# Attention values and output products in column halves, the row maxima moved into the MLP, and one score bank in four copied out by VectorE

## The chip, the core and the metric

The kernel runs on one core of one Trainium2 chip. The metric is the device time of one execution in microseconds (us). Engines: PE (TensorE, with its weight loads as PEld), ACT (ScalarE), DVE (VectorE), POOL (GpSimd) and SP (SyncE, which here only issues DMAs). A difference of about 0.2% is what a measurement of this kernel can tell from none.

## The reference, cut to what matters

```python
x = A_x                                        # [1, 2048, 448], S = 2048, D = 448
# A: 16 heads of width 28, one key and one value head for all of them
q = (x @ wq).reshape(B, S, 16, 28).transpose(0, 2, 1, 3)
k, v = x @ wk, x @ wv
p = softmax(einsum("bhqd,bkd->bhqk", q, k) * 28 ** -0.5)
a = einsum("bhqk,bkd->bhqd", p, v).transpose(0, 2, 1, 3).reshape(B, S, 448) @ wo
# B: token shift, then an MLP of width F = 1792
h  = gelu(layernorm(x) @ w1)
x1 = x + shifted_quarters(h) @ w2
b  = x1 + gelu(layernorm(x1) @ w3) @ w4
g  = sigmoid((x * gate_w).sum(-1, keepdims=True))
return g * a + (1 - g) * b
```

Everything is float32. The test data make the scores large (`wq` and `wk` are scaled by about 42 and 44), so the softmax needs a shift by something like the row maximum.

## The kernel before

All instruction streams are written out by hand: the order in which the Python code emits an engine's instructions is the order in which that engine runs them (`tc.manual_schedule` for all five engines). The kernel has three stages.

**First stage (0 to about 127 us).** Projections of queries, keys, values and gate, and the token-shift half of B. The queries go to a DRAM tensor `qd`, [4 groups, 128 partitions, 2048 positions]. A group holds four heads, each on 32 partitions: 28 query rows, and four spare rows.

**MLP (about 127 to 402 us).** For each of four blocks `b` of 512 positions, 14 iterations `f` over chunks of 128 of F. An iteration emits `w3_part(b, f)` (11 matmuls of 512 columns, then on ACT two gelus `gh`, `gf` and on DVE the low half `gl = gf - gh`), and, two iterations behind, `w4_part(f - 2, ...)` (12 matmuls of 448 columns into four accumulators). So f = 0 and f = 1 of a block have no `w4_part`. At b = 2, f = 1 the queries of the first unit are loaded and at f = 5 split into high and low halves (`q_split`); at b = 3 two "fills" compute this unit's maxima (`max_all(0)`, `max_end(0)`).

**Attention (402 us to the end).** There are NU = 16 *units*: block `b` of 512 queries times group `g` of four heads. A unit takes NV = 8 *steps*; step k = 8 u + v handles two tiles of 128 keys (kt = 2v and 2v + 1). A step emits, in this order:

- at v = 6, `q_begin(u + 2)` (DVE: a cast and a subtraction of 512 columns, `q_split`) and `q_fetch(u + 3)` (a load of 256 KB);
- for each kt, `scores`: three rounds of four matmuls. The four heads of a round use four row tiles of the array at once and write four PSUM banks. Then `exps`: ACT reads each bank, takes the exponential, and writes a tile `p` in SBUF (L810);
- at v = 2 and v = 3 the reciprocal of the last unit's row sums and its product with the output (`recip`, `norm`), through small DMAs `rt`, `rd` and the broadcast `rb`;
- at v = 2, `max_all(u + 1)` (four matmuls of the queries with 32 of the keys, and a DVE reduction) and `max_end(u + 1)` (three small DVE operations and eight DMAs that write minus the maxima, as two float32r terms, into two spare rows of the queries' SBUF tile `qh`);
- at v = 4 to 7, the output product of the last unit, `wo_job` and `wo_add`: for 128 queries eight matmul instructions of 448 columns in four column tiles, and one DVE addition into `ot`. For unit 0 `w4_job` stands in its place;
- `values` of step k - 1: `vext` (values and a column of ones) times `p`, 16 matmuls of 512 columns in four column tiles into one bank, which DVE copies or adds to `o` (L826, L828).

The maxima need not be exact: they are taken over 32 keys only, row sums beyond a limit are noted (`check`), and the branch `redo` at the end recomputes everything with full maxima in that case.

PSUM has eight banks, kept as a list: `take()` removes the first one, and it is appended again where its last reader is emitted. So a step's banks go round in a fixed order, and a bank's next user waits for its last reader: of the four banks of a key tile for the exponentials, of the bank of `values` for the DVE addition.

The hooks of this change are already there: `READ` is the order in which a key tile's four banks are read, and `DRAIN`, empty before, lists those that DVE copies to SBUF, where `late_exps` takes the exponential in place after both key tiles.

Of the kernel before, what the change touches and what calls it, by code (L numbers as in the profile page):

```python
# [9 lines left out]
F32 = mybir.dt.float32  # L10
F32R = mybir.dt.float32r
AF = mybir.ActivationFunctionType
ALU = mybir.AluOpType
# [23 lines left out]
def f32(ap):  # L37
    return ap.bitcast(F32)
# [3 lines left out]
def gated_mix_kernel(  # L42
# [44 lines left out]
    def misc_tile(name):  # L87
        return psA.tile([P, 512], F32, tag="misc", bufs=1, name=name)
# [105 lines left out]
    mx_of = {}  # L194
    mc_of = {}

# [22 lines left out]

    def max_end(u):  # L220
        mr = mx_of.pop(u).rearrange("p j t -> p (j t)")
        mc = late.tile([P, 32], F32R, tag="mc", bufs=1, name=f"mc_{u}")
        nc.vector.tensor_scalar(mc[:, 0:16], mr, -1.0, None, op0=ALU.mult)
        nc.vector.scalar_tensor_tensor(mc[:, 16:32], mr, -1.0, f32(mc)[:, 0:16],
                                       op0=ALU.mult, op1=ALU.subtract)
        mrow = late.tile([P, 32], F32, tag="mrow", bufs=1, name=f"mrow_{u}")
        nc.vector.transpose(mrow, f32(mc))
        for k in range(2):
            for p in range(4):
                r = 32 * p + 16 * k  # L230
                nc.sync.dma_start(
                    f32(qh_of[u])[DH + k:P:32, :].rearrange("j (t p q) -> p j t q", p=4, q=32)[p], mrow[r:r + 16, :])

# [368 lines left out]
    with tc.tile_pool(name="s2", bufs=1, reuse_waits="tile") as s2, \  # L602
# [4 lines left out]

        fills = [lambda: max_all(0, misc_tile("m_0")), lambda: max_end(0)]

        def fill():  # L610
            if fills:
                fills.pop(0)()

# [25 lines left out]
        for b in range(NB):  # L639
            acc = [ps2.tile([P, 512], F32, tag="acc", bufs=4, name=f"acc_{b}_{t}") for t in range(4)]  # L640
            gs = {}
            for f in range(NF):
# [40 lines left out]
            for t in range(4):  # L683
# [5 lines left out]
            for t in range(4):  # L689
# [3 lines left out]
                nc.vector.tensor_add(xt, xt, acc[t][:, 0:D])  # L693
        assert not fills
    ctx2.close()


    with tc.tile_pool(name="s3", bufs=1, reuse_waits="tile") as s3, \
# [7 lines left out]
        def take():  # L706
            return banks.pop(0)
# [48 lines left out]

        def wo_job(u, t, end=None):
            b, g = divmod(u, NG)
            n = 4 * b + t
            ps = take()  # L760
            for j in range(4):
                tok = slice(t * P + 32 * j, t * P + 32 * j + 32)
                nc.tensor.matmul(ps[32 * j:32 * j + 32, 0:D], on_of[u][:, tok], wof[:, g, :],  # L763
                                 start=True, stop=True, tile_position=(0, 32 * j))
            before = x1[:, n, :] if g == 0 else ot_of[n]
            if g == 0:
                ot_of[n] = s3.tile([P, D], F32, tag="ot", bufs=5, name=f"ot_{n}")
            if end:
                end(t, n, ps[:, 0:D], before)
                banks.append(ps)  # L770
                return
            return n, g, ps, before

        def wo_add(n, g, ps, before):
            nc.vector.scalar_tensor_tensor(ot_of[n], ps[:, 0:D], gg[:, n:n + 1], before, op0=ALU.mult, op1=ALU.add)  # L775
            banks.append(ps)
            if g == NG - 1:
                nc.sync.dma_start(out[0, n * P:(n + 1) * P, :], ot_of[n])

# [37 lines left out]
        def values(u, v, add=True):  # L817
            pv = take()
            for kt in (2 * v, 2 * v + 1):
                ps = p_of.pop((u, kt))  # L820
                for j in range(4):
                    nc.tensor.matmul(pv[32 * j:32 * j + 32, :], vext[:, kt, :], ps[j],  # L822
                                     start=(kt % 2 == 0), stop=(kt % 2 == 1), tile_position=(0, 32 * j))
            if v == 0:
                o_of[u] = s3.tile([P, 512], F32, tag="o", bufs=2, name=f"o_{u}")
                nc.vector.tensor_copy(o_of[u], pv)  # L826
            elif add:
                nc.vector.tensor_add(o_of[u], o_of[u], pv)  # L828
            else:
                return pv  # L830
            banks.append(pv)

        READ = (0, 1, 2, 3)
        DRAIN = ()
        WO_AT = (4, 5, 6, 7)
        M_AT = 2

        for k in range(NU * NV):
            u, v = divmod(k, NV)
            if v == 6 and u + 2 < NU:  # L840
                q_begin(u + 2)
                q_fetch(u + 3)
            for kt in (2 * v, 2 * v + 1):
                exps(u, kt, scores(u, kt))
            for kt in (2 * v, 2 * v + 1):
                late_exps(u, kt)
            if v == 2 and sums:
                norms.append(recip(*sums.pop()))
            if v == 3 and norms:
                norm(*norms.pop())  # L850
            if v == M_AT and u + 1 < NU:
                ps = take()
                max_all(u + 1, ps)
                banks.append(ps)
# [16 lines left out]
        pv = values(u, NV - 1, False)  # L871
# [4 lines left out]
        tq = [bank(f"oq_{t}")[:, 0:P] for t in range(4)]  # L876
        rr = s3.tile([P, 2, 2, 4], F32, name="rr4")
# [33 lines left out]
        def keep_warm(n):  # L911
            for _ in range(n):
                nc.tensor.matmul(banks[0][:, 0:256], warm[:, 0:P], warm, start=True, stop=True)

        for t in range(4):
            nc.vector.tensor_add(o[:, toks[t]], o[:, toks[t]], pv[:, toks[t]])
        with tc.block():
# [34 lines left out]
        with tc.If(again > 0, label="redo"):  # L952
            for b in range(NB):
                for g in range(NG):
# [3 lines left out]
                    max_full(u, bank)  # L958
                    max_end(u)
                    pv = take()  # L960
# [13 lines left out]
                    for t in range(4):  # L974
                        wo_add(*wo_job(u, t))

# [50 lines left out]
```

## Time and profile before

| | |
|---|---|
| median of 3 runs | 971.56 us (971.14 to 971.71) |
| the profiled execution | 970.74 us, of it 968.9 us span |
| granted PE clock, mean | 0.996 |
| PE busy | 960.1 us (99%) |
| PE weight loads (PEld) | 589.3 us (61%) |
| ACT busy | 647.0 us (67%) |
| DVE busy | 345.7 us (36%) |
| POOL busy | 74.9 us (8%) |

A busy PE is not a PE at its peak: matmuls are pipelined, their records overlap, and the interval from one start to the next is what tells the rate. In the two MLP and attention stages the limits differ: the MLP has ACT busy 25% and PEld 87% of the time, attention ACT 93% and PEld 44%.

### The profile page before, as it was taken

Reading aid. Unit: us, or ns where it says so; the run is one execution under the profiler, and the core shown is the slowest. Engines: PE = TensorE matmul, PEld = TensorE weight load, DVE = VectorE, ACT = ScalarE, POOL = GpSimd, SP = SyncE. Lnnn points to the kernel's source line nnn. Section 1 sums busy time; section 2 is a strip of 40 time slices with the busy share of each in tenths; the row PEclk is TensorE's granted clock in tenths of the full one; section 3 lists DMA queues with packets and bytes.
Section 4 is the critical chain, followed back from the end, with each engine's and each line's share of the span. In section 5 each row is a group of like instructions: output and inputs, shape, how many; then the busy total and the mean of one; then the engine's idle time right before and its main releaser. Section 6 shows DMA issues by size and latency. Waiting matters only on the chain. (4 is left out here: it accounts for less than half of the span.)

```text
span 968.9 us, 19222 instructions
## 1 busy us (share of the span) xinstructions
PE 960.1 (99%) x7571; PEld 589.3 (61%) x7571; DVE 345.7 (36%) x636; ACT 647.0 (67%) x1262; POOL 74.9 (8%) x105
## 2 busy tenths in 40 slices
PE   9999999999999999999999999999999999999996
PEld 7788888888888888644444444444444444444442
DVE  5663354433413421233333333333233332333323
ACT  5532444422222222589999999999999999999993
POOL 2242200221002400200000000000000000000000
PEclk9999999999999999999999999999999999999999
DMA  9703342300300300100000010000010000100001
GB/s 317 263 27 76 103 162 83 89 22 10 93 1 1 82 1 1 60 13 14 14 23 14 24 50 24 14 13 24 24 51 15 14 25 13 53 23 2 13 13 42
DMA packets 38753, 46.22 MB, mean 48 GB/s; under 512 B 8880, under 2 KB 27008, under 8 KB 38656
## 3 DMA queue, kind: packets, MB, share of 16 engines
q1 hardware_dynamic: 35632, 39.45, 13.6%
q10 hardware_dynamic: 3024, 5.47, 1.6%
q8 instruction: 61, 1.00, 0.4%
q14 instruction: 36, 0.29, 0.1%
HBM read 32.85 MB, written 11.67 MB: 46 GB/s over the span
## 5 line engine op out<-in xcount | busy, mean ns | idle before, releaser
L810 ACT ACTIVATE p<-bank 128x512 f32<-128x512 f32 x1024 | 510.9, 653 | 42.7 <-PE bank L800 42.7
L822 PE MATMUL bank<-p,vext 128*32 128x512 f32 x2048 | 245.9, 598 | 0.0
L800 PEld LDWEIGHTS bank<-qh,kH 30*128 30x128 f32 x1024 | 86.2, 182 | 141.8 <-ACT p L810 128.4
L800 PE MATMUL bank<-qh,kH 30*128 30x512 f32 x1024 | 168.4, 465 | 0.1
L625 ACT ACTIVATE gh<-g 128x512 fp32r<-128x512 f32 x55 | 32.8, 597 | 187.6 <-PE g L134 187.6
L800 PE MATMUL bank<-qh,kL 28*128 28x512 f32 x1024 | 137.9, 404 | 0.0
L822 PEld LDWEIGHTS bank<-p,vext 128*32 128x32 f32 x2048 | 59.9, 110 | 127.3 <-issue 101.1
L800 PE MATMUL bank<-ql,kH 28*128 28x512 f32 x1024 | 131.3, 389 | 0.0
L828 DVE TENSOR_TENSOR o<-o,bank 128x512 f32<-128x512 f32 x111 | 76.3, 687 | 123.9 <-PE bank L822 72.9
L627 DVE TENSOR_TENSOR gl<-gf,gh 128x512 fp32r<-128x512 f32 x55 | 38.3, 696 | 168.0 <-ACT gf L626 168.0
L636 PE MATMUL acc<-w4l,gh 128*128 128x448 f32 x220 | 80.4, 366 | 0.0
L635 PE MATMUL acc<-w4h,gh 128*128 128x448 f32 x220 | 80.4, 365 | 0.0
L637 PE MATMUL acc<-w4h,gl 128*128 128x448 f32 x220 | 80.3, 365 | 0.0
L800 PEld LDWEIGHTS bank<-ql,kH 28*128 28x128 f32 x1024 | 73.6, 185 | 9.6
L131 PE MATMUL g<-al,w3h 128*128 128x512 f32 x168 | 65.7, 391 | 0.0
L130 PE MATMUL g<-ah,w3h 128*128 128x512 f32 x168 | 65.6, 390 | 0.0
L132 PE MATMUL g<-ah,w3l 128*128 128x512 f32 x168 | 65.6, 390 | 0.0
L800 PEld LDWEIGHTS bank<-qh,kL 28*128 28x128 f32 x1024 | 62.1, 184 | 0.0
L763 PE MATMUL bank<-wof,on 128*32 128x448 f32 x512 | 61.2, 551 | 0.0
L775 DVE SCALAR_TENSOR_TENSOR ot<-bank,gg,ot 128x448 f32<-128x448 f32 x44 | 30.1, 684 | 85.7 <-PE bank L763 56.9
L635 PEld LDWEIGHTS acc<-w4h,gh 128*128 128x128 f32 x220 | 41.3, 188 | 4.7
L902 POOL TENSOR_TENSOR ot<-y,ot 128x448 f32<-128x448 f32 x1 | 1.2, 1162 | 553.5 <-ACT y L901 553.5
(188 smaller groups left out, 997.1 us busy)
## 6 DMA issues: line engine op xcount, KB each, us to landing
qd<-qf ACTq DMA_DIRECT2D x16, 256.0 KB
qr<-qd SPq DMA_DIRECT2D x16, 256.0 KB
rb<-rd SPq DMA_DIRECT2D x15, 256.0 KB
x<-in_x_dram SPq DMA_DIRECT2D x4, 896.0 KB
xd<-xt SPq DMA_DIRECT2D x16, 224.0 KB
w34raw<-in_w_dram SPq DMA_DIRECT2D x7, 512.0 KB
out_dram<-ot SPq DMA_DIRECT2D x15, 224.0 KB
w34raw<-in_w_dram SPq DMA_DIRECT2D x7, 448.0 KB
```

Source lines behind the costliest of these rows:

```text
L130: nc.tensor.matmul(ps, wh[:, c, :], ah[:, c, :], start=(c == 0), stop=False)
L131: nc.tensor.matmul(ps, wh[:, c, :], al[:, c, :], start=False, stop=False)
L132: nc.tensor.matmul(ps, wl[:, c, :], ah[:, c, :], start=False, stop=False)
L627: nc.vector.tensor_sub(gl, gf, f32(gh))
L635: nc.tensor.matmul(ps, gh[:, tok], w4h[i][:, k, :], start=(f == 0), stop=False)
L636: nc.tensor.matmul(ps, gh[:, tok], w4l[i][:, k, :], start=False, stop=False)
L637: nc.tensor.matmul(ps, gl[:, tok], w4h[i][:, k, :], start=False, stop=(f == stop))
L763: nc.tensor.matmul(ps[32 * j:32 * j + 32, 0:D], on_of[u][:, tok], wof[:, g, :], start=True, stop=True, tile_position=(0, 32 * j))
L800: nc.tensor.matmul(bs[j], w, a, start=(i == 0), stop=(i == 2), tile_position=(32 * j, 0))
L810: nc.scalar.activation(ps[j], bs[j], AF.Exp, scale=SCALE)
L822: nc.tensor.matmul(pv[32 * j:32 * j + 32, :], vext[:, kt, :], ps[j], start=(kt % 2 == 0), stop=(kt % 2 == 1), tile_position=(0, 32 * j))
L828: nc.vector.tensor_add(o_of[u], o_of[u], pv)
```

## The change

- **Values in halves.** `values` runs once for columns 0 to 255 and once for 256 to 511, each in a bank of its own; each half has its own DVE addition, and gives its bank back after it.
- **Output products in halves.** `wo_half` computes 224 of the 448 columns. One half stands in each step ahead of the values: the halves 0 to 3 of the last unit at v = 4 to 7, the halves 4 to 7 at v = 0 to 3 of the unit after. In the last unit the steps v = 4 to 7 have two halves.
- **All maxima in the MLP.** For u = 0 to 6 in the iterations f = 2 to 8 of b = 2, for u = 7 to 15 in f = 0 to 8 of b = 3: a load of the unit's queries, `max_cast` (DVE), `max_all`, `max_end`. In the iteration after, `max_send` writes the maxima into the spare rows of `qd` in DRAM: four DMAs from SP's queue and four from ACT's. Attention loads them with the queries.
- **One bank in four copied by DVE.** `DRAIN = (3,)`, `READ = (0, 3, 1, 2)`: ACT reads three banks of each key tile, DVE copies the fourth, and ACT takes its exponential from SBUF after both key tiles' others.
- `recip` moves from the middle of v = 2 to the end of v = 1, `norm` from the middle to the end of v = 3, both behind the values.

```diff
-    def max_end(u):
+    def max_end(u, again=False):
...
         nc.vector.transpose(mrow, f32(mc))
+        row_of[u] = mrow
+        if again:
+            max_send(u, f32(qh_of[u]), nc.sync)
+
+    def max_send(u, q, other):
+        mrow = row_of.pop(u)
         for k in range(2):
             for p in range(4):
                 r = 32 * p + 16 * k
-                nc.sync.dma_start(
-                    f32(qh_of[u])[DH + k:P:32, :].rearrange("j (t p q) -> p j t q", p=4, q=32)[p], mrow[r:r + 16, :])
+                (other if k else nc.sync).dma_start(
+                    q[DH + k:P:32, :].rearrange("j (t p q) -> p j t q", p=4, q=32)[p], mrow[r:r + 16, :])
...
-        fills = [lambda: max_all(0, misc_tile("m_0")), lambda: max_end(0)]
...
+        def max_load(u):
+            if u < NU:
+                q_load(u, s2a.tile([P, 512], F32, tag="xn", bufs=1, name=f"qm_{u}"))
+
+        def max_cast(u):
+            qh_of[u] = qh0
+            nc.vector.tensor_copy(qh0, qr_of.pop(u))
+            max_load(u + 1) if u != 6 else None
...
                 if b == 2 and f == 1:
...
+                    max_load(0)
+                u = f - 2 if b == 2 and 2 <= f <= 8 else f + 7 if b == 3 and f <= 8 else None
+                if b == 2 and f == 12:
+                    max_load(7)
+                if row_of:
+                    w, = row_of
+                    max_send(w, qd[w % NG, :, w // NG * 512:w // NG * 512 + 512], nc.scalar)
+                if u is not None:
+                    max_cast(u)
+                if b == NB - 1 and f == 11:
                     q_load(0, s2a.tile([P, 512], F32, tag="xn", bufs=1, name="qr_0"))
-                if b == 2 and f == 5:
+                if b == NB - 1 and f == 13:
                     q_split(0, qh0, ql0)
                 if f >= 2:
                     for t in range(4):
                         w4_part(f - 2, t, gs[f - 2], acc)
-                        if b > 2 and t % 2 == 0 and f < NF - 1:
-                            fill()
+                if u is not None:
+                    max_all(u, max_tile(f"m_{u}") if u % 2 else misc_tile(f"m_{u}"))
+                    max_end(u)
...
-        def wo_job(u, t, end=None):
+        def wo_job(u, t, end=None, cols=slice(0, D)):
...
-                nc.tensor.matmul(ps[32 * j:32 * j + 32, 0:D], on_of[u][:, tok], wof[:, g, :],
+                nc.tensor.matmul(ps[32 * j:32 * j + 32, cols], on_of[u][:, tok], wof[:, g, cols],
...
+        def wo_half(u, i):
+            t, h = divmod(i, 2)
+            wo_job(u, t, None, slice(224 * h, 224 * h + 224))
...
         def values(u, v, add=True):
-            pv = take()
-            for kt in (2 * v, 2 * v + 1):
-                ps = p_of.pop((u, kt))
-                for j in range(4):
-                    nc.tensor.matmul(pv[32 * j:32 * j + 32, :], vext[:, kt, :], ps[j],
-                                     start=(kt % 2 == 0), stop=(kt % 2 == 1), tile_position=(0, 32 * j))
             if v == 0:
                 o_of[u] = s3.tile([P, 512], F32, tag="o", bufs=2, name=f"o_{u}")
-                nc.vector.tensor_copy(o_of[u], pv)
-            elif add:
-                nc.vector.tensor_add(o_of[u], o_of[u], pv)
-            else:
-                return pv
-            banks.append(pv)
-
-        READ = (0, 1, 2, 3)
-        DRAIN = ()
+            pvs = []
+            for q in (slice(0, 256), slice(256, 512)):
+                pv = take()
+                for kt in (2 * v, 2 * v + 1):
+                    for j in range(4):
+                        nc.tensor.matmul(pv[32 * j:32 * j + 32, q], vext[:, kt, :], p_of[u, kt][j][:, q],
+                                         start=(kt % 2 == 0), stop=(kt % 2 == 1), tile_position=(0, 32 * j))
+                if v == 0:
+                    nc.vector.tensor_copy(o_of[u][:, q], pv[:, q])
+                elif add:
+                    nc.vector.tensor_add(o_of[u][:, q], o_of[u][:, q], pv[:, q])
+                pvs.append(pv)
+                if add:
+                    banks.append(pv)
+            return pvs
+
+        READ = (0, 3, 1, 2)
+        DRAIN = (3,)
         WO_AT = (4, 5, 6, 7)
-        M_AT = 2
...
-            if v == 2 and sums:
-                norms.append(recip(*sums.pop()))
-            if v == 3 and norms:
-                norm(*norms.pop())
-            if v == M_AT and u + 1 < NU:
-                ps = take()
-                max_all(u + 1, ps)
-                banks.append(ps)
-                max_end(u + 1)
-            job = None
-            if v in WO_AT:
-                if u:
-                    job = wo_job(u - 1, WO_AT.index(v))
-                else:
-                    w4_job(WO_AT.index(v))
-            if job:
-                wo_add(*job)
+            if u == 0 and v in WO_AT:
+                w4_job(WO_AT.index(v))
+            if v >= 4 and u:
+                wo_half(u - 1, v - 4)
+            if v < 4 and u > 1:
+                wo_half(u - 2, v + 4)
+            if v >= 4 and u == NU - 1:
+                wo_half(u - 1, v)
             if k:
                 values(*divmod(k - 1, NV))
-                if v == 0:
-                    sums.append(sums_begin(u - 1, o_of[u - 1]))
+            if u and v == 0:
+                sums.append(sums_begin(u - 1, o_of[u - 1]))
+            if u and v == 1:
+                norms.append(recip(*sums.pop()))
+            if u and v == 3:
+                norm(*norms.pop())
```

The rest of the diff fits the tail and the `redo` branch to the new functions.

More of the change, by code (lines that the diff above doesn't have):

```diff
@@ L194, in gated_mix_kernel @@
     mx_of = {}
-    mc_of = {}
+    row_of = {}
     def max_tile(name):
@@ L762, in wo_job @@
                 tok = slice(t * P + 32 * j, t * P + 32 * j + 32)
-                nc.tensor.matmul(ps[32 * j:32 * j + 32, 0:D], on_of[u][:, tok], wof[:, g, :],
+                nc.tensor.matmul(ps[32 * j:32 * j + 32, cols], on_of[u][:, tok], wof[:, g, cols],
                                  start=True, stop=True, tile_position=(0, 32 * j))
-            before = x1[:, n, :] if g == 0 else ot_of[n]
-            if g == 0:
+            if g == 0 and cols.start == 0:
                 ot_of[n] = s3.tile([P, D], F32, tag="ot", bufs=5, name=f"ot_{n}")
+            before = x1[:, n, cols] if g == 0 else ot_of[n][:, cols]
             if end:
                 end(t, n, ps[:, 0:D], before)
-                banks.append(ps)
[L771 to L775, printed above, removed]
+            else:
+                nc.vector.scalar_tensor_tensor(ot_of[n][:, cols], ps[:, cols], gg[:, n:n + 1], before,
+                                               op0=ALU.mult, op1=ALU.add)
+                if g == NG - 1 and cols.stop == D:
+                    nc.sync.dma_start(out[0, n * P:(n + 1) * P, :], ot_of[n])
             banks.append(ps)
-            if g == NG - 1:
-                nc.sync.dma_start(out[0, n * P:(n + 1) * P, :], ot_of[n])
+        def wo_half(u, i):
+            t, h = divmod(i, 2)
+            wo_job(u, t, None, slice(224 * h, 224 * h + 224))
         weigh_x1(NT - 4, NT)
@@ L846, in gated_mix_kernel @@
                 late_exps(u, kt)
[L847 to L863 removed]
+            if u == 0 and v in WO_AT:
[6 more added lines that the diff above has]
+                wo_half(u - 1, v)
             if k:
                 values(*divmod(k - 1, NV))
[L866 to L867 removed]
+            if u and v == 0:
[4 more added lines that the diff above has]
+                norm(*norms.pop())
         assert not sums and not norms
         u = NU - 1
[L871 removed]
+        pvs = values(u, NV - 1, False)
         o = o_of[u]
@@ L875, in gated_mix_kernel @@
         tp = [bank(f"ot_{i}").rearrange("p (t n) -> p t n", t=4) for i in range(2)]
-        tq = [bank(f"oq_{t}")[:, 0:P] for t in range(4)]
+        tq = [bank(f"oq_{t}") for t in range(4)]
+        spare = tq[3]
+        tq = [ps[:, 0:P] for ps in tq]
         rr = s3.tile([P, 2, 2, 4], F32, name="rr4")
@@ L912, in keep_warm @@
             for _ in range(n):
-                nc.tensor.matmul(banks[0][:, 0:256], warm[:, 0:P], warm, start=True, stop=True)
+                nc.tensor.matmul(spare[:, 0:256], warm[:, 0:P], warm, start=True, stop=True)
         for t in range(4):
-            nc.vector.tensor_add(o[:, toks[t]], o[:, toks[t]], pv[:, toks[t]])
+            nc.vector.tensor_add(o[:, toks[t]], o[:, toks[t]], pvs[t // 2][:, toks[t]])
         with tc.block():
@@ L958, in gated_mix_kernel @@
                     max_full(u, bank)
-                    max_end(u)
+                    max_end(u, True)
                     pv = take()
@@ L974, in gated_mix_kernel @@
                     for t in range(4):
[L975 removed]
+                        wo_job(u, t)
 _OUTS = [((1, S, D), "float32")]
```

4 lines of the change are left out of this document (removed).

## The prediction

> **What bounds the kernel now.** I read the page, then the busy time in windows, then attention's order of time engine by engine. The span is
>
> ```profile
> span 968.9 us, 19222 instructions
> ```
>
> and the execution 970.74 us, 1.8 us beyond it and 0.8 below the median of 971.56. One unit of attention in the windows view (columns: PE, PEld, DVE, ACT, POOL busy with instruction counts, PE clock, DMA share, GB/s), under a window early in attention, and SP's order of time, in which the query load marks the units:
>
> ```profile
> 407.80:411.10 3.30, 3.30 (x21) 0.60 (x16) 1.12 (x2) 3.28 (x7) 0.00 (x0) 0.50 0.24 53
> 573.70:608.00 34.30, 34.30 (x364) 15.14 (x360) 11.46 (x21) 31.88 (x65) 0.00 (x0) 1.00 0.08 25
> ```
> ```profile
> 602.83 0.33 SPq L178 DMA_DIRECT2D qr<-qd  x1
> 614.34 0.57 SPq L737 DMA_DIRECT2D rt<-o  x1
> 618.78 0.33 SPq L746 DMA_DIRECT2D rd<-rr  x1
> 620.44 0.53 SPq L748 DMA_DIRECT2D rb<-rd  x1
> 622.04 4.56 SPq L231 DMA_DIRECT2D qh<-mrow  x8
> 637.17 0.32 SPq L178 DMA_DIRECT2D qr<-qd  x1
> ```
>
> A unit takes 637.17 - 602.83 = 34.34 us, a step 4.29 on average. ACT is busy 93% of it, yet it isn't the limit. PE, weight loads, ACT and DVE in one step that has an output product:
>
> ```profile
> 600.86 0.51 PE L800 MATMUL bank<-qh,kH 30*128 30x512 f32 x4
> 601.20 0.41 PE L800 MATMUL bank<-qh,kL 28*128 28x512 f32 x4
> 601.43 0.40 PE L800 MATMUL bank<-ql,kH 28*128 28x512 f32 x4
> 601.66 0.64 PE L800 MATMUL bank<-qh,kH 30*128 30x512 f32 x4
> 601.89 0.65 PE L800 MATMUL bank<-qh,kL 28*128 28x512 f32 x4
> 602.14 0.62 PE L800 MATMUL bank<-ql,kH 28*128 28x512 f32 x4
> 602.69 0.96 PE L763 MATMUL bank<-wof,on 128*32 128x448 f32 x8
> 603.47 1.90 PE L822 MATMUL bank<-p,vext 128*32 128x512 f32 x16
> 605.30 0.51 PE L800 MATMUL bank<-qh,kH 30*128 30x512 f32 x4
> ```
> ```profile
> 603.09 0.13 PEld L822 LDWEIGHTS bank<-p,vext 128*32 128x32 f32 x4 [0.25 <-ACT p L810]
> 603.47 0.13 PEld L822 LDWEIGHTS bank<-p,vext 128*32 128x32 f32 x4 [0.25 <-issue]
> 603.90 0.13 PEld L822 LDWEIGHTS bank<-p,vext 128*32 128x32 f32 x4 [0.30 <-issue]
> ```
> ```profile
> 601.91 4.03 ACT L810 ACTIVATE p<-bank 128x512 f32<-128x512 f32 x8 [0.40 <-PE bank L800]
> 606.35 0.60 ACT L810 ACTIVATE p<-bank 128x512 f32<-128x512 f32 x1 [0.41 <-PE bank L800]
> ```
> ```profile
> 601.06 0.69 DVE L828 TENSOR_TENSOR o<-o,bank 128x512 f32<-128x512 f32 x1 [1.02 <-ACT p L810]
> ```
>
> The step lasts 605.30 - 600.86 = 4.44: scores 1.83 (to 602.69), product 0.78, values 1.83, with PE's queue in order throughout. ACT's eight exponentials follow each other at about (4.03 - 0.60)/7 = 0.49, or 3.92 a step, and ACT then waits 0.4 for scores. So PE's chain sets the product steps. Two things in it can go. The second key tile's rounds stretch from 0.41 to 0.64, because one matmul of the four is late: its bank is that of the values, and DVE's addition ends at 601.06 + 0.69 = 601.75. And the steps are uneven: four of eight carry 0.78 of product, which leaves the others 34.34 - 4 x 4.44 = 16.6 or 4.15 each, maxima and `norm`'s waits included: near ACT's 3.92.
>
> **Attention after.** DVE's rows by length, for the halves and the copies:
>
> ```profile
> L828 DVE TENSOR_TENSOR o<-o,bank x111: 678/687/689, 416.1 to 952.9; 128x512 f32<-128x512 f32 x111
> L826 DVE COPY o<-bank x16: 690/691/693, 411.8 to 926.9; 128x512 f32<-128x512 f32 x16
> L753 DVE TENSOR_TENSOR on<-o,rb x15: 691/692/694, 453.7 to 934.0; 128x512 f32<-128x512 f32 x15
> L916 DVE TENSOR_TENSOR o<-o,bank x4: 280/280/288, 954.6 to 955.2; 128x128 f32<-128x128 f32 x4
> ```
>
> A line through 128 and 512 columns gives 0.42 for an addition of 256. Let S be the step's first score round.
>
> *Scores.* Without the late matmul the rounds start 0.34, then 0.23 apart, the last at S + 1.26. The product followed the last matmul (602.14 + 0.62 - 0.40 = 602.36) by 0.33, the change from row to column tiles, so PE could go on at S + 1.59. But the product's bank is the one that the first exponential empties: it starts 1.05 after S (601.91 against 600.86, 606.35 against 605.30), takes 0.60, and I add 0.05 for the release: S + 1.70. The late matmul itself goes: the last half's addition starts some 0.2 after the next S (now 601.06, for values whose last round is twice as long) and ends by 0.62, before the bank is due at about 0.7.
>
> *Product, half.* Two rounds of 0.40 (602.69 to 603.09, its start included) and 0.38 for 448 columns become 0.21 + 0.19 = 0.40 for 224.
>
> *Values.* Rounds take 0.38 for 448 columns and 0.43 for 512: in proportion, with no fixed part that shows. Eight rounds of 256 then take what four of 512 did, 1.73, and with the way back to scores (605.30 - 603.47 - 4 x 0.43 = 0.11) 1.84. The other end is 0.23 a round, the score rounds' interval: these are the nearest that have eight instructions (four loads, four matmuls) in so short a time. That would add 0.11 to the values and 0.06 to the product. I take the proportion, since it comes from the same form of matmul.
>
> Sum: 1.70 + 0.40 + 1.84 = **3.94 a step**, against ACT's 3.92. Two of ACT's eight now read SBUF; less than 0.49 each wins nothing, as ACT isn't the limit; were they 0.60, a whole unoverlapped instruction, ACT would need 4.14. I take 0.49. They give ACT 0.98 of work that needs no new scores, and so cover most of the 1.05 from S to the first exponential.
>
> *DVE.* Per step two copies (1.38), two halves of addition (0.84) and a product half (about 0.4) make 2.6 of 3.94. The copies wait for scores, and behind them stand the product's and the values' additions; the first copy ends at S + 1.05 + 0.69 + 0.05 = 1.79, its bank is due for the values at 1.70 + 0.40 = 2.10. `norm` (0.69 from 0.62 on) still lets it end by 2.05. `q_begin` at v = 6 (cast 0.43, subtraction 0.69) runs to S + 1.74, the copy then to 2.48: **0.38 lost once a unit**. `recip` reads `rt` a whole step after its issue (rd's write was followed by rb's issue in 1.66), and `norm` stands two steps behind `recip`: no DVE wait; at worst one of some 0.5 a unit. SP loses the eight sends (4.56 a unit), so nothing queues ahead of these.
>
> A unit is 8 x 3.94 + 0.38 = 31.9, less 2.44. Thirteen units (2 to 14): -31.7. Unit 1 has no products in four steps, which ACT then holds at 3.92: 31.8, -2.5. Unit 15 has twice the halves in four steps, 8 x 3.94 + 4 x 0.40 = 33.1, and had no maxima to lose before: I take -0.3 (between 0 and the -1.2 against 34.34). Unit 0 starts badly:
>
> ```profile
> 407.91 0.43 DVE L183 CAST qh<-qr 128x512 fp32r<-128x512 f32 x1 [5.05 <-DMA qr<-qd]
> ```
> ```profile
> 411.58 0.19 PEld L800 LDWEIGHTS bank<-qh,kH 30*128 30x128 f32 x4 [1.30 <-ACT p L810]
> ```
> ```profile
> 404.27 1.48 PE L800 MATMUL bank<-qh,kH 30*128 30x512 f32 x3
> ```
>
> `q_begin(1)` holds DVE for its load until 407.91 and to 409.1 in all; behind it now queue the first copies, and behind these PE's second step, which needs the copied bank: 409.8, then 1.70 + 1.84 to the third step, 413.4 against 411.58. So +1.8, less 0.8 for its six other steps (0.13 of late matmul each): +1.0. Attention: **-33.5**.
>
> **MLP after.** One set of maxima stands there now:
>
> ```profile
> 342.33 0.36 PE L635 MATMUL acc<-w4h,gh 128*128 128x448 f32 x1
> 342.53 0.37 PE L636 MATMUL acc<-w4l,gh 128*128 128x448 f32 x1
> 342.74 0.36 PE L637 MATMUL acc<-w4h,gl 128*128 128x448 f32 x1
> 342.94 0.56 PE L203 MATMUL m<-khd,qh 128*128 128x128 f32 x4
> ```
> ```profile
> 342.53 0.60 ACT L625 ACTIVATE gh<-g 128x512 fp32r<-128x512 f32 x1 [1.41 <-PE g L134]
> ```
> ```profile
> 347.98 0.60 ACT L625 ACTIVATE gh<-g 128x512 fp32r<-128x512 f32 x1 [4.36 <-PE g L134]
> 348.47 0.59 ACT L626 ACTIVATE gf<-g 128x512 f32<-128x512 f32 x1
> 352.92 0.60 ACT L625 ACTIVATE gh<-g 128x512 fp32r<-128x512 f32 x1 [3.85 <-PE g L134]
> ```
> ```profile
> 343.65 0.69 DVE L627 TENSOR_TENSOR gl<-gf,gh 128x512 fp32r<-128x512 f32 x1 [1.80 <-ACT gf L626]
> ```
>
> The iteration with maxima takes 347.98 - 342.53 = 5.45, the next 4.94: 0.51 each, fifteen more: +7.7. Here PE has no slack. New is a wait: `max_cast` stands on DVE behind `gl`, which ends at 344.34. The cast (0.43), the gap before it (0.03), the release (0.05) and a weight load's share (0.1) let the maxima start at 344.95. Twelve `w4` matmuls from 342.33 at 0.205 end at 344.79, so 14 iterations lose 0.16: +2.3. At b = 3, f = 0 and 1, however, no `w4_part` stands between, and PE would go on at 342.33: it waits 2.62, twice, with the next `w3_part` queued behind: +5.2. The early window above shows PE's clock at 0.50 for 3.3 us, after a stretch in which single score matmuls came 0.49 apart (three in 1.48, row 404.27). I expect one such stretch from the two waits, which halves some 3.4 us: +1.7 (0 to 3.4).
>
> The Trainium skill (TensorE: Matmul & The Clock Gate, "Why this matters for your kernels") asks for PE-idle gaps over about 3 us before the clock falls; by that rule 2.62 would cost nothing, and the time would be 1.7 lower. The trace has a fall with no such gap, so the row decides.
>
> The rest hides: sends of 0.57, four on SP and four on ACT (2.3 us, behind the gelus that use 1.1 of each iteration; next gelus queue behind them, with over 1 us to spare), a query load per iteration, reduction and small operations on DVE behind `gl`. If that cover failed, a late gelu would still have one iteration before `w4_part` reads it. MLP: **+16.9**.
>
> **Sum:** 970.74 - 33.5 + 16.9 = 954.1, and 0.8 to the median: **955 us**.
>
> **Rivals.**
>
> *A fixed cost per round.* Half rounds at 0.23: 0.17 a step, 124 steps (15.5 units), +21: 976 in full, 965 at half that price. For it speaks that a score round takes 0.23 for 512 columns, where each of the two passes that values make over theirs takes half of 0.43; against it the proportion of 0.38 to 0.43.
>
> The Trainium skill (TensorEngine Tiling (Array Packing), "Instruction Overhead") gives each matmul some 60 cycles of overhead. As an estimate of mine from that page, 25 ns on each of five more rounds a step would give 970. The rows for 448 and 512 columns show no such part.
>
> *PE's instructions become the bound (slower).* A unit has 724 PE instructions in 34.3 us, 47 ns each. After, a step has 48 for scores, 16 for the product and 64 for values: 128. At 3.94 that is 31 ns each, sustained. The score rounds show 29 (eight in 0.23), but only in bursts. It decides from about 32 ns, where attention's gain equals the MLP's cost; at 34 ns a step takes 4.35, +51: 1006.
>
> *The MLP's waits don't show* and `q_begin` finds slack (cast early enough, no slow clock): 2.3, 1.7 and 5 less: 946.
>
> **Chances.** Forecast 0.53 (own range 949 to 962), fixed cost 0.18 (0.06, 0.05 and 0.07 on the three outcomes), instruction bound 0.16, no waits 0.13. Faster by over 0.2% (about what a measurement can tell from no change): 0.53 + 0.13 + 0.06 = 0.72; within: 0.05; slower: 0.16 + 0.07 = 0.23. The range reaches from the no-waits case to the fixed cost: 944 to 973, and leaves out the instruction bound.
>
> **What would show it.** Right: units of about 32 us; copied banks off ACT; PE waiting for the first exponential ahead of the product; value rounds 0.21 to 0.22 apart; iterations of 5.6 with maxima, and two PE gaps of 2.6 us at b = 3. Wrong: rounds at 0.23 or more, gaps inside the values with the wait named "issue", DVE's copies as last releaser in every step, or an MLP longer by more than 20 us.

## The result, and the profile after

The changed kernel takes 957.99 us (median of four runs, 955.28 to 958.90) against 971.35 for the kernel before (four runs): ratio 0.986, 95% interval 0.9841 to 0.9879, so 1.4% shorter. The prediction was 955, range 944 to 973. The profiled execution takes 957.32 us, 955.5 of it span.

One unit of attention in the windows view (PE, PEld, DVE, ACT, POOL busy with counts, PE clock, DMA share, GB/s), and the query loads in SP's order of time:

```profile
590.00:621.90 31.90, 31.52 (x520) 18.54 (x512) 22.55 (x47) 31.79 (x65) 0.00 (x0) 1.00 0.11 34
```
```profile
612.99 0.33 SPq L178 DMA_DIRECT2D qr<-qd  x1
...
644.87 0.32 SPq L178 DMA_DIRECT2D qr<-qd  x1
```

A unit takes 644.87 - 612.99 = 31.88, where 34.34 stood. The DMAs of maxima are gone from SP's queue, DVE's share rose from a third to 71%, and ACT's busy time per unit is the same: the copies did not lighten ACT, they only changed what it waits for. One step, PE, ACT and DVE in order of time:

```profile
623.38 0.51 PE L820 MATMUL bank<-qh,kH 30*128 30x512 f32 x4
623.71 0.40 PE L820 MATMUL bank<-qh,kL 28*128 28x512 f32 x4
...
624.18 0.40 PE L820 MATMUL bank<-qh,kH 30*128 30x512 f32 x4
...
624.64 0.41 PE L820 MATMUL bank<-ql,kH 28*128 28x512 f32 x4
625.09 0.58 PE L782 MATMUL bank<-wof,on 128*32 128x224 f32 x8
625.49 1.91 PE L845 MATMUL bank<-p,vext 128*32 128x256 f32 x32
627.33 0.50 PE L820 MATMUL bank<-qh,kH 30*128 30x512 f32 x4
```
```profile
623.35 1.21 ACT L835 ACTIVATE p<-p 128x512 f32<-128x512 f32 x2
624.44 3.05 ACT L830 ACTIVATE p<-bank 128x512 f32<-128x512 f32 x6
627.31 1.20 ACT L835 ACTIVATE p<-p 128x512 f32<-128x512 f32 x2
628.40 0.60 ACT L830 ACTIVATE p<-bank 128x512 f32<-128x512 f32 x1
```
```profile
623.57 0.42 DVE L850 TENSOR_TENSOR o<-o,bank 128x256 f32<-128x256 f32 x1 [0.50 <-ACT p L830]
624.48 1.39 DVE L828 COPY p<-bank 128x512 f32<-128x512 f32 x2 [0.49 <-PE bank L820]
625.82 0.45 DVE L790 SCALAR_TENSOR_TENSOR ot<-bank,gg,x 128x224 f32<-128x224 f32 x1
```

The step is 627.33 - 623.38 = 3.95. The second key tile's rounds no longer stretch (0.40, where 0.64 stood): no score matmul is late. The first exponential starts 1.06 after the scores, the product 0.65 after that, the values 0.40 after the product, the next scores 1.84 after the values. The product's weight loads name what it waited for, the bank of that first exponential:

```profile
625.09 0.16 PEld L782 LDWEIGHTS bank<-wof,on 128*32 128x32 f32 x8 [0.47 <-ACT p L830]
```

ACT meanwhile fills the time up to its first exponential with the two from SBUF (627.31).

DVE's groups bear out the lengths that the prediction took for copies and halves:

```profile
L828 DVE COPY p<-bank 128x512 f32<-128x512 f32 x256 | 175.1, 690 | 45.5 <-PE bank L820 44.7
L850 DVE TENSOR_TENSOR o<-o,bank 128x256 f32<-128x256 f32 x222 | 93.5, 421 | 93.1 <-PE bank L845 49.2 <-ACT p L830 43.9
```

The beginning of b = 3 in the MLP, PE, ACT and DVE:

```profile
345.46 0.89 PE L203 MATMUL m<-khd,qh 128*128 128x128 f32 x4 [2.40 <-DVE qh L620]
...
347.10 0.63 PE L132 MATMUL g<-ah,w3l 128*128 128x512 f32 x1
347.53 0.63 PE L130 MATMUL g<-ah,w3h 128*128 128x512 f32 x1
...
352.59 1.08 PE L203 MATMUL m<-khd,qh 128*128 128x128 f32 x4 [2.33 <-DVE qh L620]
```
```profile
343.10 0.60 ACT L634 ACTIVATE gh<-g 128x512 fp32r<-128x512 f32 x1 [5.44 <-PE g L134]
...
350.30 0.60 ACT L634 ACTIVATE gh<-g 128x512 fp32r<-128x512 f32 x1 [6.12 <-PE g L134]
...
357.39 0.60 ACT L634 ACTIVATE gh<-g 128x512 fp32r<-128x512 f32 x1 [6.01 <-PE g L134]
```
```profile
344.21 0.69 DVE L636 TENSOR_TENSOR gl<-gf,gh 128x512 fp32r<-128x512 f32 x1 [3.03 <-ACT gf L635]
344.82 0.49 DVE L620 CAST qh<-qm 128x512 fp32r<-128x512 f32 x1
```

PE waits 2.40 and 2.33 us for the cast behind `gl`, and behind each wait the matmuls come 0.43 apart in place of 0.23: PE's granted clock is 0.5 for 3.41 us, twice (345.67 to 349.08 and 352.50 to 355.91). The two iterations take 7.20 and 7.09 where 2.49 stood.

The beginning of attention, DVE, PE and the windows view:

```profile
426.41 0.43 DVE L183 CAST qh<-qr 128x512 fp32r<-128x512 f32 x1 [4.95 <-DMA qr<-qd]
...
427.48 1.28 DVE L828 COPY p<-bank 128x512 f32<-128x512 f32 x2
```
```profile
428.21 0.80 PE L820 MATMUL bank<-qh,kH 30*128 30x512 f32 x3 [5.33 <-DVE p L828]
...
429.24 1.05 PE L820 MATMUL bank<-qh,kH 30*128 30x512 f32 x4
...
431.08 3.56 PE L845 MATMUL bank<-p,vext 128*32 128x256 f32 x32
434.56 0.51 PE L820 MATMUL bank<-qh,kH 30*128 30x512 f32 x4
```
```profile
427.50:430.90 3.40, 2.69 (x23) 1.86 (x23) 1.95 (x4) 2.63 (x5) 0.00 (x0) 0.50 0.32 77
430.90:434.40 3.50, 3.50 (x35) 1.38 (x32) 1.12 (x2) 2.66 (x6) 0.00 (x0) 0.50 0.02 5
```

The first copies stand on DVE behind `q_begin(1)`, which waits 4.95 us for its load; PE stands empty for 5.33, and from inside this gap on its clock is at half for 10.2 us (424.2 to 434.4): values that take 1.84 elsewhere take 3.48.

### The profile page after: what moved, and what is told of

It reads as the page before. It is cut to its first block, busy times and chain, and to the rows that moved or that the text cites. A ratio compares the mean times of both kernels' runs of the same rounds, so it can differ in the third digit from the quotient of the medians.

```text
span 955.5 us, 24595 instructions
## 1 busy us (share of the span) xinstructions
PE 928.2 (97%) x10099; PEld 651.6 (68%) x10099; DVE 549.2 (57%) x1095; ACT 645.6 (68%) x1262; POOL 74.5 (8%) x105
## 5 line engine op out<-in xcount | busy, mean ns | idle before, releaser
L830 ACT ACTIVATE p<-bank 128x512 f32<-128x512 f32 x768 | 391.4, 628 | 9.1 <-PE bank L820 7.4
L845 PE MATMUL bank<-p,vext 128*32 128x256 f32 x4096 | 247.0, 382 | 2.1 <-ACT p L830 1.7
L828 DVE COPY p<-bank 128x512 f32<-128x512 f32 x256 | 175.1, 690 | 45.5 <-PE bank L820 44.7
L845 PEld LDWEIGHTS bank<-p,vext 128*32 128x32 f32 x4096 | 131.1, 110 | 91.9 <-DVE p L828 6.9
L835 ACT ACTIVATE p<-p 128x512 f32<-128x512 f32 x256 | 154.2, 687 | 3.4 <-DVE p L828 3.4
L850 DVE TENSOR_TENSOR o<-o,bank 128x256 f32<-128x256 f32 x222 | 93.5, 421 | 93.1 <-PE bank L845 49.2
L820 PE MATMUL bank<-qh,kH 30*128 30x512 f32 x1024 | 119.0, 445 | 5.3 <-DVE p L828 5.3
L820 PE MATMUL bank<-qh,kL 28*128 28x512 f32 x1024 | 106.1, 393 | 0.0
L820 PE MATMUL bank<-ql,kH 28*128 28x512 f32 x1024 | 105.4, 390 | 0.0
L782 PE MATMUL bank<-wof,on 128*32 128x224 f32 (+1 forms) x992 | 73.1, 370 | 5.2 <-ACT p L830 0.4
```

The lines of the kernel that those rows point to most:

```text
L782: nc.tensor.matmul(ps[32 * j:32 * j + 32, cols], on_of[u][:, tok], wof[:, g, cols], start=True, stop=True, tile_position=(0, 32 * j))
L820: nc.tensor.matmul(bs[j], w, a, start=(i == 0), stop=(i == 2), tile_position=(32 * j, 0))
L828: nc.vector.tensor_copy(ps[j], bs[j])
L830: nc.scalar.activation(ps[j], bs[j], AF.Exp, scale=SCALE)
L835: nc.scalar.activation(p_of[u, kt][j], p_of[u, kt][j], AF.Exp, scale=SCALE)
L845: nc.tensor.matmul(pv[32 * j:32 * j + 32, q], vext[:, kt, :], p_of[u, kt][j][:, q], start=(kt % 2 == 0), stop=(kt % 2 == 1), tile_position ...
```

## Experiments

| run | median us | ratio to before, 95% | a usual step | a unit |
|---|---|---|---|---|
| before | 971.35 | 1 | 4.29 (mean) | 34.34 |
| changed kernel | 957.99 | 0.9841 to 0.9879 | 3.96 | 31.90 |
| e6_maxima_alone | 977.78 | 1.0050 to 1.0081 | 4.22 (mean) | 33.75 |
| e3_no_copies | 1006.15 (one run) | - | 4.43 | 35.41 |
| e5_products_whole | 976.25 | 1.0037 to 1.0070 | 3.96 and 4.33 | 33.15 |
| e4_values_whole | 964.75 | 0.9905 to 0.9943 | 4.01 | 32.43 |
| e7_half_late_exps | 952.95 (one run) | - | 3.945 | 31.82 |
| e1_cast_early | 953.16 | 0.9798 to 0.9832 | 3.96 | 31.93 |
| e2_second_query_later | 952.88 | 0.9794 to 0.9832 | 3.96 | 31.92 |
| e8_both_early | 947.85 | 0.9737 to 0.9800 | 3.96 | 31.93 |
| e9_two_rows | 945.51 | 0.9722 to 0.9749 | 3.96 | 31.92 |
| e10_split_low_later | 941.78 | 0.9689 to 0.9724 | 3.96 | 31.67 |
| e11_rows_elsewhere | 939.84 | 0.9672 to 0.9699 | 3.96 | 31.67 |

**The maxima alone.** The kernel before, with only the maxima moved into the MLP.

> The kernel before with one part of the change alone: all maxima in the MLP and loaded with the queries; values and products whole, no bank copied by VectorE. Prediction's terms: the MLP grows by 17 as in the changed kernel; attention loses the eight sends, the reduction and the four matmuls of v = 2, whose step falls from about 4.5 to 3.9-4.0: 14 units x 0.5 to 0.9 = 7 to 13 less. So 975 to 982: slower than before, with PE's chain of 4.44 in the four product steps untouched. Rival (the maxima had slowed the steps around them too, and their removal alone brings most of attention's gain): units under 33 us and 969 or less.

977.78, slower than before by 0.5 to 0.8%. The MLP grows by 16.7 us, a usual unit falls by 0.59 and the step v = 2 from 4.52 to 3.92. So what the move costs is not repaid by what it takes out of attention; the gain comes from the other three parts, which use DVE's time. Whether these three would gain as much with the maxima left in attention was not tried, nor was the move of `recip` and `norm` by itself.

**Without the copies.**

```diff
-        READ = (0, 3, 1, 2)
-        DRAIN = (3,)
+        READ = (0, 1, 2, 3)
+        DRAIN = ()
```

> The changed kernel without copies by VectorE: READ = (0, 1, 2, 3), DRAIN = (), all else kept. Theory (a loop: scores, first exponential, release of its bank, product, values, scores; ScalarE can only work ahead in it on the exponentials of copied banks): ScalarE idles from S to S + 1.05 in each step, has all eight exponentials behind it, and the values wait for the last of them: steps of 4.3 to 4.7, plus 0.35 to 0.75 on 124 steps, 1000 to 1050. Rival (ScalarE's eight exponentials set the step wherever they read from): steps of 3.9 to 4.0 and about 958, or less, since those from SBUF take 0.52 against 0.48.

1006.15, steps of 4.43. ACT's order of time:

```profile
603.21 4.03 ACT L830 ACTIVATE p<-bank 128x512 f32<-128x512 f32 x8 [0.40 <-PE bank L820]
607.62 4.03 ACT L830 ACTIVATE p<-bank 128x512 f32<-128x512 f32 x8 [0.39 <-PE bank L820]
```

Eight exponentials, then a wait of 0.40 for new scores in every step. The size is as expected, the way not quite: ACT does not idle from the scores to its first exponential (606.21 to 607.62, 1.41), but works on the last exponentials of the step before until 607.24, and one of the next scores' first four matmuls waits 0.31 for a bank that these have to empty (606.79). Halves without copies (4.43) are worse than everything whole (4.22, the run before this). Unit 1 shows where that lies: its steps without a product take 3.70, 4.22, 3.92 and 3.97, as in the run with the maxima alone (3.68, 4.22, 3.92, 3.96), and a half costs a step as much here (4.43) as a whole product did there (4.43 in three steps of four), in twice as many steps. The copies are worth 48 us here, by one run.

**Products whole, and values whole.**

```diff
-                wo_half(u - 1, v - 4)
-            if v < 4 and u > 1:
-                wo_half(u - 2, v + 4)
...
+                wo_job(u - 1, v - 4)
```

> The changed kernel with whole output products (448 columns) in the steps v = 4 to 7 in place of a half in every step. In the run with half of the copied banks' exponentials left out, unit 1's steps without a product took 3.58 and those with half a product 3.94, so the loop through TensorE is 3.55 + 0.40 for a half; with all exponentials both took 3.96, so ScalarE's own work sets 3.96. Theory (two limits that nearly meet, loop and ScalarE): steps without a product stay at 3.96 (ScalarE), steps with a whole one take 3.55 + 0.78 = 4.33 or 4.34: 0.37 x 4 x 14 units, about 20 to 21 more: 978 to 979. Rival (one average limit: what a step saves the next can use): steps of 3.96 throughout, 958 to 960.

```diff
-            for q in (slice(0, 256), slice(256, 512)):
+            for q in (slice(0, 512),):
```

> The changed kernel with the values whole: four rounds of 512 columns into one bank, one addition of 0.69 us on VectorE in place of two of 0.42; the rest is kept. Theory (the halves' use is that the first bank comes free early, so that no score matmul is late; a round costs in proportion to its columns): the values keep 1.84, the late score matmul returns, and a step grows by 0.05 to 0.13: 4.01 to 4.09, 964 to 974. Rival (halving does nothing, since ScalarE's work of 3.96 sets the step and the loop has room for the late matmul): steps of 3.94 to 3.98, 956 to 960. Second rival (each round has a fixed cost, so that fewer rounds are cheaper): steps under 3.9, under 952.

Whole products: 976.25. Steps v = 1 to 3 take 3.96, v = 5 to 7 4.33, as the theory says; the first step without a product, v = 0, takes 3.57, as the loop alone would, and the first with one, v = 4, 4.72: 0.39 less and 0.39 more, so the sum is the same. The 0.24 lost at v = 6 is gone in the longer step, hence 2 us less than expected. Halving is worth 18.3 us. One whole product:

```profile
616.20 0.51 PE L820 MATMUL bank<-qh,kH 30*128 30x512 f32 x4
...
617.92 0.96 PE L782 MATMUL bank<-wof,on 128*32 128x448 f32 x8
618.69 1.91 PE L845 MATMUL bank<-p,vext 128*32 128x256 f32 x32
620.53 0.50 PE L820 MATMUL bank<-qh,kH 30*128 30x512 f32 x4
```

Product 0.77, against 0.40 for a half; scores and values as in the changed kernel.

Whole values: 964.75, steps of 4.01, at the lower edge of what the theory gave. The late score matmul is back (the second key tile's rounds show 0.58 again):

```profile
622.45 0.51 PE L820 MATMUL bank<-qh,kH 30*128 30x512 f32 x4
...
623.24 0.58 PE L820 MATMUL bank<-qh,kH 30*128 30x512 f32 x4
...
624.61 1.90 PE L845 MATMUL bank<-p,vext 128*32 128x512 f32 x16
626.44 0.51 PE L820 MATMUL bank<-qh,kH 30*128 30x512 f32 x4
```

The values themselves take 1.83 whole and 1.84 in halves: a round has no fixed part.

**Loop or ScalarE?** The exponentials from SBUF on half of their columns; this kernel leaves out the other half:

```diff
-                nc.scalar.activation(p_of[u, kt][j], p_of[u, kt][j], AF.Exp, scale=SCALE)
+                nc.scalar.activation(p_of[u, kt][j][:, 0:256], p_of[u, kt][j][:, 0:256], AF.Exp, scale=SCALE)
```

> The exponentials that ScalarE takes from SBUF (two of eight in each step) cover only columns 0 to 255 of 512, so half of the copied banks' exponentials are left out; the rest is the changed kernel. They take 0.52 us each now, and about 0.3 in this form, so ScalarE has 0.45 less to do in a step of 3.96. Theory (the step is set by a loop through TensorE: first exponential, release of its bank, product, values, next scores): the step stays at 3.93 to 3.97 and the time at 955 to 959. Rival (ScalarE, busy 99.6% and with 3.90 of work a step, sets the step): the step falls to 3.5-3.6, and the time by 40 to 50, to about 910.

952.95, in one run some 2 us below what the theory gave; steps with a half product 3.945, so the loop sets them and ACT now waits:

```profile
605.13 3.05 ACT L830 ACTIVATE p<-bank 128x512 f32<-128x512 f32 x6 [0.32 <-PE bank L820]
608.01 0.77 ACT L835 ACTIVATE p<-p 128x256 f32<-128x256 f32 x2
609.08 3.04 ACT L830 ACTIVATE p<-bank 128x512 f32<-128x512 f32 x6 [0.30 <-PE bank L820]
```

But unit 1's steps without a product fell from 3.96 to 3.58. Both theories hold, each for its steps: the loop allows 3.58 without a product and 3.945 with a half, ACT's own work allows 3.96. In the changed kernel the two nearly coincide.

**The cast earlier.** In the MLP:

```diff
+                if u is not None:
+                    max_cast(u)
                 gs[f] = w3_part(b, f)
...
-                if u is not None:
-                    max_cast(u)
```

> In the MLP max_cast is emitted ahead of w3_part, so that on VectorE it stands in front of gl instead of behind it; the rest is the changed kernel. Theory (the maxima's matmuls wait for a cast that queues behind gl): the iterations with maxima go from 5.46-5.61 us to 5.45, and f = 0 and f = 1 of b = 3 from 7.20 and 7.09 to about 2.49 + 0.51 = 3.0, and no stretch at half clock is left in the MLP. That is 8.3 for the two and about 1.4 for the other 14: about 948 us. Rival (the two long iterations come from the sends of the maxima or from the load of the queries, not from the place of the cast): under 2 us gained, 956 or more. Rival (the half clock is not the consequence of the wait): the waits of 2.40 and 2.33 go, but 3.4 us at half clock stay and the two iterations keep about 1.7 each: about 952.

953.16: 4.8 gained, of 9.7 expected. Neither the half clock nor the two long waits are left (f = 0 and 1 take 3.28 and 3.96), so the half clock was a consequence of the waits. The time lies near the 952 of the second rival, but only by chance, since the half clock that this rival kept is gone. What is missing is elsewhere: four other iterations of b = 3 now take 5.84 to 7.00. DVE says why:

```profile
357.16 0.21 DVE L227 STREAM_TRANSPOSE mrow<-mc 128x32 f32<-128x32 f32 x1 [2.77 <-DMA qd<-mrow]
357.29 0.38 DVE L620 CAST qh<-qm 128x512 fp32r<-128x512 f32 x1
357.59 0.68 DVE L636 TENSOR_TENSOR gl<-gf,gh 128x512 fp32r<-128x512 f32 x1
```

The transpose into `mrow`, of which there is one buffer, waits until the sends of the unit before have read it. In the changed kernel this wait hid behind everything else; with the cast behind it, `gl` and PE wait too.

**The second query later.** `q_begin(1)` and `q_fetch(2)` move from the start of attention into its fourth step.

```diff
-        q_begin(1)
-        q_fetch(2)
...
+            if k == 3:
+                q_begin(1)
+                q_fetch(2)
```

> q_begin(1) and q_fetch(2) move from the start of attention to its fourth step (q_fetch(1) stays); the rest is the changed kernel. Theory (the first step's copies of banks queue on VectorE behind a cast that waits 4.95 us for its load, and the emptied array then runs 10.2 us at half clock): the third step starts about 7.5 us behind the first instead of 13.8, and steps 4 to 7 of the first unit (4.4 to 4.8 now) keep what w4_job costs: 5 to 6.5 us gained, about 952. Rival (the start of attention is slow because a new stage begins at a low clock whatever VectorE does): half clock again, gain under 2 us. The cast now stands in the fourth step with its load long in, and costs there what it costs at v = 6, 0.24.

952.88, as expected. PE's order of time, the first and the third step:

```profile
421.97 0.51 PE L818 MATMUL bank<-qh,kH 30*128 30x512 f32 x4
...
429.45 0.50 PE L818 MATMUL bank<-qh,kH 30*128 30x512 f32 x4
```

429.45 - 421.97 = 7.48, with 13.83 before the edit; no half clock there. The two in the MLP are still in this kernel, as they should be.

**Both, and what followed.**

> The two edits before it together (the cast ahead of w3_part; the second unit's query split in the fourth step). If the two losses are independent, the gains add: 958 - 9.7 - 5.8 = 942 to 943 us, below both kernels. If the earlier cast moves the end of the MLP so that the first query load of attention becomes late, part is given back: 945 to 948.

947.85: the two measured gains, 4.8 and 5.1, add. This lies in the second expectation's range, but not for its reason: the first unit takes 33.33 us with and without the earlier cast, so no load became late there. The loss to the transposes stays, 27.1 us of waiting in eight times. No half clock is left ahead of the last microseconds. Next, two buffers for `mrow`:

```diff
-        mrow = late.tile([P, 32], F32, tag="mrow", bufs=1, name=f"mrow_{u}")
+        mrow = late.tile([P, 32], F32, tag="mrow", bufs=2, name=f"mrow_{u}")
```

> The two early edits together, and two buffers instead of one for mrow, the tile from which the maxima are sent. In the version with the two edits the iterations of b = 3 took 4.82 to 6.91 us, since the transpose into mrow waited 27.1 us in eight times for the sends of the unit before, and the cast and gl now queue behind it on VectorE. Theory (that buffer is the whole of it): the iterations with maxima go to 5.39 and the first two of b = 3 to 3.0, 6.5 us less: about 941 us. Rival (the send queues themselves, 2.5 to 5.2 us of issuing in each iteration on SyncE and on ScalarE, are the limit): the wait moves to the query load or to the gelus, and 2 us or less is gained: 946 or more.

945.51, 2.3 less and between the two expectations. The waits for sends are gone but for 1.1 us. Two things keep it from 941. The first four iterations of b = 3 take 2.97, 4.89, 4.73 and 5.12, 0.9 more than twice 3.0 and twice 5.4: there the cast waits for its load (1.17 us at most) and a gelu stands behind sends on ACT's queue. And the usual iterations of all four blocks take 4.98 to 5.03 in place of 4.94, with maxima 5.43 to 5.45. First, though, the stall at v = 6:

```diff
-            if v == 6 and u + 2 < NU:
-                q_begin(u + 2)
+            if v == 5 and u + 2 < NU:
+                q_cast(u + 2)
+            if v == 6 and u + 2 < NU:
+                q_low(u + 2)
```

> The version with two buffers for mrow, and in attention q_begin is divided: its cast (0.42 us) at v = 5, its subtraction (0.69) at v = 6. Theory (the 0.24 that v = 6 loses is the copy of a bank queued on VectorE behind 1.11 us of q_begin; norm, 0.69 at the same place, costs nothing at v = 4): both steps take 3.96, 13 x 0.24 = 3.1 us less: about 938. Rival (v = 6 is long for another reason, such as the query load that is issued there): v = 6 stays at 4.20, no gain.

941.78, 3.7 less for 3.1 expected (the 938 counted from the 941 that the run before missed): v = 6 takes 3.96, as `norm`'s step does with an operation as long ahead of the copies. Last, `mrow` in another pool, so that no other tile moves:

```diff
-        mrow = late.tile([P, 32], F32, tag="mrow", bufs=2, name=f"mrow_{u}")
+        mrow = (late.tile([P, 32], F32, tag="mrow", bufs=1, name=f"mrow_{u}") if again else
+                s2a.tile([P, 32], F32, tag="mrow2", bufs=2, name=f"mrow_{u}"))
```

> As the version with the divided q_begin, but the two buffers of mrow stand at the end of the MLP's own tile pool, so that no other tile moves in SBUF. In the two versions with the second buffer in the older pool, every iteration of the MLP took 4.98 to 5.02 us in place of 4.94, also in blocks 0 and 1 where no maxima are sent, and those with maxima 5.43 to 5.45 in place of 5.39. Theory (the 128 bytes by which the second buffer moved the other tiles cost this): 4.94 and 5.39 again, 2.0 to 2.5 us less: about 939.5. Rival (the second buffer's sends or something else in these versions costs it): 4.98 to 5.02 stays, and 941 to 943.

939.84, 1.9 less, ratio to before 0.9686 (0.9672 to 0.9699): the iterations take 4.94 and 5.39 again. The intervals of the last two runs overlap, so the profiles decide: from the first gelu to the first scores the MLP takes 279.71, where it took 281.94. This is the best version found: below the changed kernel by 18 us, and below the kernel before by 31.

## Why the prediction came out as it did

**Steps and units: right.** Forecast 1.05 + 0.65 + 0.40 + 1.84 = 3.94 a step and 31.9 a unit; measured 1.06 + 0.65 + 0.40 + 1.84 and 31.90. The product does wait for the bank of the first exponential, the late matmul is gone with its cause (values whole bring it back), and rounds cost by their columns (values whole 1.83, in halves 1.84). Thirteen units gave 31.8 us (forecast 31.7), unit 1 2.46 (2.5), the last unit and the tail 1.0 (0.3).

**"ACT isn't the limit": half wrong.** The prediction took 3.92 for ACT's eight. Its own rate is 3.96 (the run with whole products: steps without one), so ACT sets the step as much as the loop does. The forecast lost nothing by it, which is luck: the two are some 0.02 apart; whoever shortens only the loop from here on wins nothing.

**`q_begin` at v = 6: cause right, size wrong.** 0.24 a unit, not 0.38: the cast started 0.53 after the scores, where the prediction had the last addition end at 0.62, and the values waited for the copy behind it, as forecast:

```profile
612.88 1.28 DVE L828 COPY p<-bank 128x512 f32<-128x512 f32 x2
```
```profile
613.61 1.45 PEld L845 LDWEIGHTS bank<-p,vext 128*32 128x32 f32 x32 [0.46 <-DVE p L828]
```

The divided version removes all of it.

**Unit 0: the term that failed most.** Forecast +1.0, measured +3.3. The order on DVE was as described, but the step "1.70 + 1.84 to the third step" was costed at full clock. Third step 13.83 behind the first, forecast 11.3. The trace of before had shown half clock at this very place, and the edit put a gap of 5.33 ahead of it, where before single score matmuls had run 0.49 apart.

**MLP: +17.3 for +16.9, a match by luck, since two errors offset.** The 14 usual iterations lost 0.61 each against the row without maxima (forecast 0.51 + 0.16). The two waits were 2.40 and 2.33 (2.62), but each brought its own stretch of half clock, where one was forecast: 9.3 us in the two iterations for 7.9.

**The sum.** 954.1 was to be compared with 957.32: attention 1.5 short, MLP 0.4, and 1.3 from the first stage, which the change does not touch: the MLP's first gelu came at 130.1 in the profile of before, 131.4 after, and between 130.7 and 133.1 in the experiments' profiles.

**The rivals.** A fixed cost per round: none, the values take 1.83 whole and 1.84 in halves. The prediction's estimate from the Trainium skill (TensorEngine Tiling (Array Packing), "Instruction Overhead"), 970, added 25 ns to each of five further rounds a step, and fails with it. PE's instruction rate: 128 in 3.95, 31 ns each, with no gap in the values; where it would bind was not reached. The waits of the MLP: they show.

**The clock.** PE's clock fell to 0.5 behind waits of 2.40 and 2.33 us, and did not where the earlier cast took them away. The Trainium skill (TensorE: Matmul & The Clock Gate, "Why this matters for your kernels") names gaps over about 3 us; here less sufficed, so the measurement decides. How long the clock stays down does not follow from the wait alone: in the run with the maxima alone, waits of 2.38 and 2.33 us brought one stretch of 6.83 and none behind the second, and gaps of 5.33 and 5.24 at the start of attention brought 10.24 in the changed kernel and 6.83 with whole values. What decides the length is not shown.

## What to carry to other kernels

When a loop over two engines is bound by a hand-over, give the engine that waits some work that needs no new data: here two exponentials from SBUF, at the price of copies on an engine that had time. An instruction moved in an engine's queue holds up whatever waits behind it: every long stall here (`max_cast` behind `gl`, copies behind `q_begin`, `gl` behind the transpose) was found by asking who stands behind a waiting instruction, and cured by order or by one more buffer. Whether spreading work evenly over the steps pays depends on what bounds them: the product halves won 18 us with the copies, and without them the mean step was 4.43, against 4.22 with whole products in half of the steps.

## What was not expected of the hardware

**Where tiles lie.** Adding one buffer of 128 bytes per partition slowed the usual iterations of the MLP from 4.94 us to 4.98 to 5.03, 2.2 us in all, also in blocks that send no maxima; both buffers at the end of a later pool cost nothing. Which tiles' new addresses matter was not tried.

**ScalarE without rest.** Exponentials from PSUM start 0.477 us apart, but when ScalarE never waits each lasts longer than the one before. The first, and the last two, of six in a row, in the run with whole products:

```profile
633.75 0.69 ACT L830 ACTIVATE p<-bank 128x512 f32<-128x512 f32 x1
```
```profile
635.66 1.22 ACT L830 ACTIVATE p<-bank 128x512 f32<-128x512 f32 x2
```

The first ends at 634.44, the sixth at 636.88: 0.488 an exponential is what it delivers, while one that starts after a wait lasts 0.60. Those from SBUF in place start 0.52 apart. So rows of starts alone, 3.90 for the eight, understate ACT's step of 3.96.
